# A fused attention and two-layer feed-forward kernel: a second staging buffer for spare weights, and a longer pipeline in the attention's first ten pairs

## The chip, the cores and the metric

The kernel runs on one core of a Trainium2 chip. A core has TensorE (PE: matmuls; PEld are its weight loads), VectorE (DVE), ScalarE (ACT), GpSimd (POOL) and SyncE (SP), which issues all DMAs here. The metric is the device time of one execution in microseconds (us), as the median of some runs.

## What is computed

Windowed attention with bias, then two feed-forward layers, in float32:

```python
scores = q @ k^T / 8 + bias; keep = (8 global keys) | (96 keys before the row)
a = softmax(where(keep, scores, -1e9)); x = a @ v      # 2 x 8 heads, 768 x 64
h = x @ w_in1;  x = (max(h,0) + alpha*min(h,0)) @ w_out1   # 1536 x 512, d_ff 2048
h = x @ w_in2;  out = (P(h) / (Q(h) + 1e-6)) @ w_out2      # P cubic, Q quadratic
```

## The kernel before, in words

**Attention.** A step z (0 to 47) is one block of 128 query rows and two heads, and a pair u (0 to 23) is two steps. A pair goes through these stages: `scores` (TensorE, L423), `biased` (VectorE adds the bias out of PSUM and keeps the row extremes, L440), `exponentials` (ScalarE, with row sums, L450), the reciprocals of the sums (`inverse`, L462: GpSimd adds 1e-9, L464, VectorE inverts, L465), `normalise` (GpSimd scales the probabilities, L470), `transpose_p` (TensorE, L486) and `copy_p` (PSUM to SBUF, L494: VectorE for every fourth step up to step 16, else ScalarE), `values` (TensorE, L505), and `store_x` (ScalarE writes the high part L526, VectorE the low part L527). Probabilities have six buffers (two steps each to three pairs), transposed ones four.

**Order.** All is written out by hand; each engine takes its own instructions in program order. Pairs 0 to 9 run in `alone(u)` (L569): scores u, reciprocals of step 2u-1 (`one_ready`), biased u, loads (`fetches`, SP), values u-2, exponentials of step 2u, store u-2, the transposes and splits of new q and k blocks, reciprocals of step 2u, a tick, exponentials of step 2u+1, transposes and copies of pair u-1, a tick. Pairs 10 to 23 share the engines with the first layer: slot s (0 to 15, `joint_slot`, L848) is pair u = 10 + s. It calls `opening` (L605: scores, reciprocals of pair u-1, biased, loads, values u-2, exponentials, store), then `first(s)` (12 matmuls of 128x512, one PSUM bank), a tick, `turning` (L623: transposes and copies of pair u-1, new inputs), `leaky(s)` (VectorE L744 and L745 read the bank, ScalarE L746, GpSimd L747), `second(s-1)` (12 matmuls) and a tick. Slots from 16 on are feed-forward alone.

**Weights.** Each weight piece (512 KB of 64-bit words) is loaded to a stage, scaled on ScalarE (L324), joined on VectorE (L313 to L315) and split into a high part (L301 on ScalarE in the slots, L303 on GpSimd in `alone`) and a low part (VectorE, L304). `tick` (L284) is one step of that: it issues the DMAs of the piece before (`spill`, L209), casts the high part of the present one and starts the next. A plan fixes at which tick a piece starts. Eight pieces, those of chunks 8 to 11, have no slot in SBUF yet (`slot is None`): they are split into `self.part[1:3]` and sent to DRAM. Their plan numbers are 15 and 17 to 23; one starts in each slot from 5 to 12 and is cast at the end of the slot after, 6 to 13.

```python
self.spill()
x = words(self.dx[n % 3])
if slot is None:
    hi, lo = (t.bitcast(F32R) for t in self.part[1:3])
```

Of the kernel before, what the change touches and what calls it, by code (L numbers as in the profile page):

```python
# [8 lines left out]
F32 = mybir.dt.float32  # L9
F32R = mybir.dt.float32r  # L10
# [3 lines left out]
ALU = mybir.AluOpType  # L14
# [3 lines left out]
P = 128  # L18
# [4 lines left out]
DM = 512  # L23
# [14 lines left out]
JOIN = 20  # L38
# [22 lines left out]
class Kernel:  # L61
# [222 lines left out]
    def tick(self, on_act, start, spread=False):  # L284
        nc = self.nc
        if self.later:
            self.later.popleft()()
        while self.splits:
            self.splits.popleft()()
        self.join_step(5)  # L290
        if self.pipe and self.pipe[0][0] == "joined":
            _, n = self.pipe.popleft()
            m, fc, kind, slot = self.plan[n]
            self.spill()
            x = words(self.dx[n % 3])
            if slot is None:
                hi, lo = (t.bitcast(F32R) for t in self.part[1:3])
            else:
                hi, lo = (flat(self.slots[slot][kind, part]) for part in PARTS)
            if on_act:  # L300
                nc.scalar.copy(hi, x)  # L301
            else:
                nc.gpsimd.tensor_scalar(hi, x, 1.0, 1.0, ALU.mult, ALU.mult)  # L303
            self.splits.append(lambda: nc.vector.tensor_sub(lo, x, hi.bitcast(F32)))  # L304
            if m == 0 and fc < KEPT:
                for part, of in zip(PARTS, (hi, lo)):
                    self.unspilled.append((words(self.spilled[fc][kind, part]), of.bitcast(F32)))
        if self.pipe:
            _, n = self.pipe[0]
            self.pipe[0] = "joined", n  # L310
            low, e, y = self.staged(n)[:, :, :, 0], self.de[n % 2].bitcast(I32), self.dx[n % 3]
            self.join += [
                lambda: nc.vector.tensor_scalar(y, e, 3, None, ALU.logical_shift_left),  # L313
                lambda: nc.vector.scalar_tensor_tensor(y, e, -(2**31), y, ALU.bitwise_and, ALU.bitwise_or),  # L314
                lambda: nc.vector.scalar_tensor_tensor(y, low, 29, y, ALU.logical_shift_right, ALU.bitwise_or),  # L315
                self.load_more,
            ]
        if not spread:
            self.join_step(5)
        if start:  # L320
            n = self.started
            self.started += 1
            self.pipe.append(("scaled", n))
            nc.scalar.mul(self.de[n % 2], self.staged(n)[:, :, :, 1].bitcast(F32), 2.0**-112)  # L324
# [37 lines left out]
    def attention_window(self, pool, moe):  # L362
# [10 lines left out]
        rec = [pool.tile([P, 4], F32, name=f"rec{i}") for i in range(2)]  # L373
        pt = [pool.tile([P, 2, 2, P], F32, name=f"pt{i}") for i in range(4)]
        self.first_saved = [pool.tile([P, DM], F32, name=f"first{d}") for d in range(NC)]

        def load(nm, i):
            if 2 <= i < NBLK:
# [80 lines left out]
                    accum_out=st[:, 4 + j : 5 + j],  # L459
                )  # L460

        def inverse(u, rows):  # L462
            r = rec[u % 2][:, rows]
            nc.gpsimd.tensor_scalar(r, stat[u % 3][:, 4:8][:, rows], 1e-9, 1.0, ALU.add, ALU.mult)  # L464
            nc.vector.reciprocal(r, r)  # L465

        def normalise(z):
            w, p, r, e = width(z), prob[z % 6], rec[z // 2 % 2], 2 * (z % 2)
            for j in range(2):
                nc.gpsimd.tensor_scalar(p[:, j, :w], p[:, j, :w], r[:, e + j : e + j + 1], 1.0, ALU.mult, ALU.mult)  # L470

        def one_ready(z):
            if z >= 0:
                inverse(z // 2, slice(2 * (z % 2), 2 * (z % 2) + 2))
                normalise(z)

        def both_ready(u):
            if steps_of(u):
                inverse(u, slice(0, 4))
                for z in steps_of(u):  # L480
                    normalise(z)

# [3 lines left out]
        def transpose_p(u, first_bank):  # L486
            for z in steps_of(u):
                w, p, t = width(z), prob[z % 6], transposed(z, first_bank + z % 2)
                for j in range(2):
                    nc.tensor.transpose(t[:, j, 0], p[:, j, w - P : w], ident)  # L490
                    if w == WIN:
                        nc.tensor.transpose(t[:, j, 1], p[:, j, 0:P], ident)
# [12 lines left out]
        def values(u):  # L505
            for z in steps_of(u):
                i, c = divmod(z, 4)
                w, p = width(z), pt[z % 4]
                o = vbank[:, c]
                for ch in range(1 if w == P else 2):  # L510
                    for j in range(2):
                        h = 2 * c + j
                        if ch == 0:
                            nc.tensor.matmul(o[HALF[j]], va[i % 4][:, h], p[:, j, 0], start=True, stop=w == P)
                        else:
                            nc.tensor.matmul(
                                o[HALF[j]], vb[i % 3][:, h], p[: NPREV + NG, j, 1], start=False, stop=True
                            )


        def store_x(u):
            if steps_of(u):
                g, off = divmod(u // 2 * P, GT)
                cs = (near, far)[u % 2]
                hi, lo = (x[g][:, cs, off : off + P] for x in (self.xhi, self.xlo))
                nc.scalar.copy(hi, vbank[:, cs])  # L526
                return lambda: nc.vector.tensor_sub(lo, vbank[:, cs], hi.bitcast(F32))  # L527
            return lambda: None
# [13 lines left out]
        def fetches(u):  # L542
            for z in (2 * u, 2 * u + 1):
                for lead, fetch in (
                    (KL, lambda i: load("k", i)),
                    (QL, lambda i: load("q", i)),
                    (VL, load_va),
                    (BL, load_vb),
                ):
                    if (z + lead) % 4 == 0:  # L550
                        fetch((z + lead) // 4)
# [17 lines left out]
        def alone(u):  # L569
            t = 2 * u - JOIN  # L570
            scores(u)
            one_ready(2 * u - 1)
            biased(u)
            if u < 2:
                later_masks(range(4 * u, 4 * u + 4))
                for _ in range(2 * KEEP):
                    nc.tensor.matmul(banks[2][:, 0:P], ident, ident, start=True, stop=True)
            fetches(u)
            values(u - 2)
            exponentials(2 * u)  # L580
            lows = [store_x(u - 2)]
            for n, (nm, i, cs) in enumerate(inputs(u)):
                bank = (3, 2)[n % 2]
                transpose_in(nm, i, bank, cs)
                lows.append(split_in(nm, i, bank, cs))
                if u < 2:
                    lows.pop()()
            keys_of_all(u)
            one_ready(2 * u)
            self.tick(False, t in self.starts, spread=True)  # L590
            exponentials(2 * u + 1)
            transpose_p(u - 1, 6)
            for low in lows:
                low()
            self.join_step(3)
            copy_p(u - 1, 6)
            self.tick(False, t + 1 in self.starts, spread=u < JOIN // 2 - 1)
            if u == 1:
                self.moe_constants()
            if u == 6:  # L600
                self.moe_constants_ready()
            if 2 * u in WL:
                self.load_next()

        def opening(u):  # L605
            scores(u)
            keys_of_all(u)
            if u == JOIN // 2:
                one_ready(2 * u - 1)
            else:  # L610
                both_ready(u - 1)
            biased(u)
            fetches(u)
            values(u - 2)
            some = steps_of(u)
            for z in some[:1]:
                exponentials(z)
            low = store_x(u - 2)
            for z in some[1:]:
                exponentials(z)  # L620
            low()

        def turning(u):  # L623
            transpose_p(u - 1, 0)
            lows = []
            for nm, i, cs in inputs(u):
                transpose_in(nm, i, 2, cs)
            copy_p(u - 1, 0)
            for nm, i, cs in inputs(u):
                lows.append(split_in(nm, i, 2, cs))  # L630
            return lows
# [6 lines left out]
    def attention_any(self, pool, moe):  # L638
# [16 lines left out]
        pt = pool.tile([P, NB, P], F32, name="a_pt")  # L655
        st = pool.tile([P, 4], F32, name="a_st")
        self.first_saved = [pool.tile([P, DM], F32, name=f"a_first{d}") for d in range(NC)]

        def transposed(dst, scale, nm, i):
            self.load_tokens(nm, i, ra)  # L660
# [317 lines left out]
```

## Time and profile before

| | |
|---|---|
| three runs | 677.8 us median (676.52 to 678.18) |
| the profiled execution | 678.08 us, its span 676.2 us |
| busy in the span | PE 631.6 us (93%), DVE 541.6 (80%), ACT 374.7 (55%), POOL 195.2 (29%) |
[...]
| pairs 0 to 9 | first scores at 8.49 us; first scores of slot 0 at 60.47 us |
| slots 9 to 15 | 150.78 to 219.60 us |

The span runs from the first to the last instruction; the execution has 1.88 us around it. Busy time says how full an engine is, not what the others wait for. That is read from the rows in which an instruction names the idle time before it and what ended it, in brackets, and from the chain of work that ended last.

### The profile page before, as it was taken

To read this page: it belongs to the slowest core of one execution; us is meant where nothing else is said; L and a number is where in the kernel's file an instruction comes from. 1 tells how busy PE (TensorE), PEld (TensorE's weight loads), DVE (VectorE), ACT (ScalarE), POOL (GpSimd) and SP (SyncE) were. 2 spreads that over 40 slices of the span, in tenths; PEclk is the share of its full clock that TensorE was granted. 3 is DMA by queue.
4 is the path that set the end of the run, shared out by engine and by line. 5 is a ranking of instruction groups with operands and counts; after the bars stand their busy time and mean duration, and the time that the engine had idled before them with its cause. 6 is when DMAs were issued, how large, how long until landed. Compare 5 with 4: busy or idle time off the path is not lost.

```text
span 676.2 us, 9567 instructions
## 1 busy us (share of the span) xinstructions
PE 631.6 (93%) x3250; PEld 510.2 (75%) x3250; DVE 541.6 (80%) x982; ACT 374.7 (55%) x782; POOL 195.2 (29%) x278
## 2 busy tenths in 40 slices
PE   7767998998988999999999998999999999999994
PEld 6656766776866888888888876888878888888782
DVE  3687789984654998876879999999999877786984
ACT  2775565665552432333324367777777766766662
POOL 4554334333232322222222212222222222222221
PEclk9897999998999999999999999999999999999997
DMA  8969488876667882331342231121110000300302
GB/s 164 198 165 271 136 249 251 258 221 222 186 225 235 291 317 89 99 121 31 126 155 63 70 117 31 32 95 39 55 62 1 1 1 1 124 1 0 126 0 69
DMA packets 84860, 82.83 MB, mean 123 GB/s; under 512 B 45312, under 2 KB 61952, under 8 KB 84800
## 3 DMA queue, kind: packets, MB, share of 16 engines
q1 hardware_dynamic: 84800, 82.11, 40.5%
q8 instruction: 28, 0.46, 0.3%
q14 instruction: 32, 0.26, 0.1%
HBM read 60.21 MB, written 19.92 MB: 119 GB/s over the span
## 4 chain that ended last, share of the span: by engine, by line
PE 59%; DVE 23%; ACT 6%; DMA 4%; issue 3%; POOL 3%; SPq 0%; DVEq 0%; ACTq 0%; POOLq 0%
PE bank L804 29%; PE bank L738 28%; DVE dx L314 3%; DVE dx L315 3%; DVE dx L313 3%; ACT prob L453 2%; DMA dwouthi_f<-part 2%; DVE prob L446 1%; DVE act L745 1%; DVE act L744 1%; DMA dwinhi_f<-part 1%; DVE xlo L527 1%; DVE klo L407 1%; DVE act L782 1%; POOL glo L747 1%
## 5 line engine op out<-in xcount | busy, mean ns | idle before, releaser
L747 POOL TENSOR_TENSOR glo<-act,ghi 128x512 fp32r<-128x512 f32 x48 | 65.6, 1367 | 225.6 <-ACT ghi L746 202.6
L789 POOL TENSOR_TENSOR glo<-act,ghi 128x512 fp32r<-128x512 f32 (+1 forms) x49 | 65.7, 1340 | 202.1 <-ACT ghi L785 187.2
L746 ACT CAST ghi<-act 128x512 fp32r<-128x512 f32 x48 | 29.8, 621 | 107.6 <-DVE act L745 99.7
L738 PE MATMUL bank<-xhi,winhi_f 128*128 128x512 f32 x256 | 68.4, 389 | 0.0
L738 PE MATMUL bank<-xhi,winlo_f 128*128 128x512 f32 x256 | 68.4, 389 | 0.0
L738 PE MATMUL bank<-xlo,winhi_f 128*128 128x512 f32 x256 | 68.4, 389 | 0.0
L453 ACT ACTIVATE prob<-prob,stat 128x232 f32<-128x232 f32 (+1 forms) x96 | 44.6, 466 | 38.8 <-DVE stat L446 38.7
L738 PEld LDWEIGHTS bank<-xhi,winhi_f 128*128 128x128 f32 x256 | 48.0, 188 | 10.0
L738 PEld LDWEIGHTS bank<-xlo,winhi_f 128*128 128x128 f32 x256 | 48.0, 188 | 10.0
L738 PEld LDWEIGHTS bank<-xhi,winlo_f 128*128 128x128 f32 x256 | 48.0, 188 | 10.0
L315 DVE SCALAR_TENSOR_TENSOR dx<-stage,dx 128x512 int32<-128x512 int32 x64 | 53.5, 836 | 2.2
L314 DVE SCALAR_TENSOR_TENSOR dx<-de,dx 128x512 int32<-128x512 int32 x64 | 51.8, 809 | 2.2
L756 ACT ACTIVATE stage<-bank 128x512 f32<-128x512 f32 (+1 forms) x49 | 28.8, 588 | 37.5 <-PE bank L738 37.4
L765 DVE SCALAR_TENSOR_TENSOR stage<-stage,abs_b 128x512 f32<-128x512 f32 (+1 forms) x49 | 36.2, 739 | 16.3 <-ACT stage L757 16.3
L470 POOL TENSOR_SCALAR prob<-prob,rec 128x232 f32<-128x232 f32 (+1 forms) x96 | 43.0, 464 | 21.7 <-DVE rec L465 14.3
L785 ACT CAST ghi<-act 128x512 fp32r<-128x512 f32 (+1 forms) x49 | 30.1, 614 | 26.5 <-DVE act L782 26.4
L324 ACT ACTIVATE de<-stage 128x512 f32<-128x512 f32 x64 | 42.4, 667 | 2.3 <-DMA stage<-in_moe_w_out_dram 2.3
L804 PE MATMUL bank<-wouthi_f,ghi 128*128 128x512 f32 x144 | 41.3, 392 | 0.6 <-ACT ghi L785 0.6
L744 DVE TENSOR_SCALAR act<-bank,al 128x512 f32<-128x512 f32 x48 | 35.8, 745 | 7.4 <-PE bank L738 7.2
L804 PE MATMUL bank<-wouthi_f,glo 128*128 128x512 f32 x144 | 41.2, 391 | 0.1
L804 PE MATMUL bank<-woutlo_f,ghi 128*128 128x512 f32 x144 | 41.0, 389 | 0.0
L313 DVE TENSOR_SCALAR dx<-de 128x512 int32<-128x512 int32 x64 | 38.0, 594 | 3.5 <-ACT de L324 3.5
(206 smaller groups left out, 1483.5 us busy)
## 6 DMA issues: line engine op xcount, KB each, us to landing
stage<-in_moe_w_in_dram SPq DMA_DIRECT2D x32, 512.0 KB, 4.1
stage<-in_moe_w_out_dram SPq DMA_DIRECT2D x32, 512.0 KB, 4.0
part<-saved_f SPq DMA_DIRECT2D x16, 256.0 KB, 4.3
va<-in_v_dram SPq DMA_DIRECT2D x13, 256.0 KB, 5.0
saved_f<-part SPq DMA_DIRECT2D x12, 256.0 KB, 3.7
out_dram<-part SPq DMA_DIRECT2D x11, 256.0 KB, 2.1
rawk<-in_k_dram SPq DMA_DIRECT2D x10, 256.0 KB, 4.7
rawq<-in_q_dram SPq DMA_DIRECT2D x10, 256.0 KB, 4.6
```

Source lines behind the costliest of these rows:

```text
L313: lambda: nc.vector.tensor_scalar(y, e, 3, None, ALU.logical_shift_left),
L314: lambda: nc.vector.scalar_tensor_tensor(y, e, -(2**31), y, ALU.bitwise_and, ALU.bitwise_or),
L315: lambda: nc.vector.scalar_tensor_tensor(y, low, 29, y, ALU.logical_shift_right, ALU.bitwise_or),
L324: nc.scalar.mul(self.de[n % 2], self.staged(n)[:, :, :, 1].bitcast(F32), 2.0**-112)
L453: nc.scalar.activation(p[:, j - e, :w], p[:, j - e, :w], AF.Exp, bias=st[:, j : j + 1], scale=-1.0, accum_out=st[:, 4 + j : 5 + j],)
L470: nc.gpsimd.tensor_scalar(p[:, j, :w], p[:, j, :w], r[:, e + j : e + j + 1], 1.0, ALU.mult, ALU.mult)
L738: nc.tensor.matmul(bk, w["in", a][:, c, :], x[:, c, :], start=e == 0, stop=e == len(seq) - 1)
L744: nc.vector.tensor_scalar(t, h, 0.0, self.al[:, fc : fc + 1], ALU.min, ALU.mult)
L747: nc.gpsimd.tensor_tensor(lo, t, hi.bitcast(F32), ALU.subtract)
L765: nc.vector.scalar_tensor_tensor(w, w, self.ab[:, 0:1], ab, ALU.add, ALU.mult)
L789: nc.gpsimd.tensor_tensor(lo, u, hi.bitcast(F32), ALU.subtract)
L804: nc.tensor.matmul(y[d], lhs, rhs, start=begin and e == 0, stop=last and e == 2)
```

## The change

It gives the spare pieces a second pair of buffers, `self.spare`, chosen by the parity of the plan number n. In `alone(u)` the reciprocals of both steps of pair u-1 are taken together, after scores u; transposes and copies are those of pair u-2, values and stores those of pair u-3, and values stand before the loads. Slot 0 then transposes and copies two pairs (8 and 9; pair 8 through banks 4 and 5), and slot 1 takes the values of two pairs (8 and 9) and stores both.

```diff
             if slot is None:
-                hi, lo = (t.bitcast(F32R) for t in self.part[1:3])
+                hi, lo = (t.bitcast(F32R) for t in (self.part[1:3], self.spare)[n % 2])
...
+        self.spare = [pool.tile([P, DM], F32, name=f"spare{d}") for d in range(2)]
...
-        def inverse(u, rows):
-            r = rec[u % 2][:, rows]
-            nc.gpsimd.tensor_scalar(r, stat[u % 3][:, 4:8][:, rows], 1e-9, 1.0, ALU.add, ALU.mult)
-            nc.vector.reciprocal(r, r)
...
-        def one_ready(z):
-            if z >= 0:
-                inverse(z // 2, slice(2 * (z % 2), 2 * (z % 2) + 2))
-                normalise(z)
...
         def both_ready(u):
             if steps_of(u):
-                inverse(u, slice(0, 4))
+                r = rec[u % 2]
+                nc.gpsimd.tensor_scalar(r, stat[u % 3][:, 4:8], 1e-9, 1.0, ALU.add, ALU.mult)
+                nc.vector.reciprocal(r, r)
...
         def alone(u):
             t = 2 * u - JOIN
             scores(u)
-            one_ready(2 * u - 1)
+            both_ready(u - 1)
             biased(u)
...
+            values(u - 3)
             fetches(u)
-            values(u - 2)
             exponentials(2 * u)
-            lows = [store_x(u - 2)]
+            lows = [store_x(u - 3)]
...
             keys_of_all(u)
-            one_ready(2 * u)
             self.tick(False, t in self.starts, spread=True)
             exponentials(2 * u + 1)
-            transpose_p(u - 1, 6)
+            transpose_p(u - 2, 6)
...
-            copy_p(u - 1, 6)
+            copy_p(u - 2, 6)
...
         def opening(u):
             scores(u)
             keys_of_all(u)
-            if u == JOIN // 2:
-                one_ready(2 * u - 1)
-            else:
-                both_ready(u - 1)
+            both_ready(u - 1)
             biased(u)
+            due = {JOIN // 2: (u - 3,), JOIN // 2 + 1: (u - 3, u - 2)}.get(u, (u - 2,))
+            for v in due:
+                values(v)
             fetches(u)
-            values(u - 2)
...
-            low = store_x(u - 2)
+            lows = [store_x(v) for v in due]
...
         def turning(u):
+            if u == JOIN // 2:
+                transpose_p(u - 2, 4)
             transpose_p(u - 1, 0)
...
+            if u == JOIN // 2:
+                copy_p(u - 2, 4)
             copy_p(u - 1, 0)
```

## Rows read from the trace of the kernel before

**Rows 1.** Chain that ended last, by line, whole span: share of the span.

```profile
PE bank L804 29%; PE bank L738 28%; DVE dx L314 3%; DVE dx L315 3%; DVE dx L313 3%; ACT prob L453 2%; DMA dwouthi_f<-part 2%; DVE prob L446 1%; DVE act L745 1%; DVE act L744 1%; DMA dwinhi_f<-part 1%; DVE xlo L527 1%; DVE klo L407 1%; DVE act L782 1%; POOL glo L747 1%
```

**Rows 2.** ScalarE's waits, 130 to 212 us: total us, times, longest us.

```profile
ACT part L301 <- DMA dwouthi_f<-part: 10.0, 3, 3.5
ACT part L301 <- DMA dwinhi_f<-part: 8.9, 3, 3.0
```

**Rows 3.** Busy us by stretch, slots 9 to 15; last columns TensorE clock, DMA share, GB/s.

```profile
150.78:164.75 13.97, 10.71 (x66) 8.43 (x66) 6.81 (x19) 7.96 (x20) 3.66 (x7) 0.88 0.52 173
164.75:173.65 8.90, 8.90 (x66) 7.30 (x65) 5.33 (x16) 4.79 (x14) 2.83 (x6) 1.00 0.77 253
173.65:182.11 8.46, 8.46 (x62) 6.86 (x61) 4.24 (x15) 4.92 (x14) 3.24 (x6) 1.00 0.73 249
...
213.00:219.60 6.60, 6.60 (x41) 5.47 (x41) 1.87 (x3) 1.38 (x4) 1.52 (x2) 1.00 1.01 337
sum 68.82, PE 61.53 PEld 47.71 DVE 34.05 ACT 32.00 POOL 21.02; mean PE 8.79 PEld 6.82 DVE 4.86 ACT 4.57 POOL 3.00
```

**Rows 4.** ScalarE in order of time, slots 8 to 10: start, us, instruction, [idle before <-releaser].

```profile
156.94 0.62 ACT L301 CAST part<-dx 128x512 fp32r<-128x512 f32 x1 [3.41 <-DMA dwouthi_f<-part]
167.23 0.62 ACT L301 CAST part<-dx 128x512 fp32r<-128x512 f32 x1 [2.98 <-DMA dwinhi_f<-part]
168.31 0.48 ACT L453 ACTIVATE prob<-prob,stat 128x232 f32<-128x232 f32 x1
```

**Rows 5.** VectorE in order of time, slots 10 and 11.

```profile
165.94 0.18 DVE L465 RECIPROCAL rec<-rec 128x4 f32<-128x4 f32 x1 [1.79 <-POOL rec L464]
166.32 0.08 DVE L446 DVE_READ_ACCUMULATOR2_ANT stat<- 128x1 f32 x1
...
176.23 0.18 DVE L465 RECIPROCAL rec<-rec 128x4 f32<-128x4 f32 x1 [1.79 <-POOL rec L464]
```

**Rows 6.** TensorE in order of time, pair 1 and slot 9.

```profile
20.23 0.60 PE L490 MATMUL bank<-part,prob 128*128 128x128 f32 x4
...
159.82 0.66 PE L399 MATMUL bank<-part,rawk 128*128 128x128 f32 x4 [3.26 <-DVE xlo L527]
```

**Rows 7.** GpSimd in order of time, pairs 0 and 1, and slot 0.

```profile
15.69 0.19 POOL L464 TENSOR_SCALAR rec<-stat 128x2 f32<-128x2 f32 x1
16.99 0.19 POOL L464 TENSOR_SCALAR rec<-stat 128x2 f32<-128x2 f32 x1
...
72.36 1.28 POOL L747 TENSOR_TENSOR glo<-act,ghi 128x512 fp32r<-128x512 f32 x1 [8.13 <-ACT ghi L746]
```

**Rows 8.** VectorE in order of time, pairs 1, 2 and 7, and slot 0.

```profile
17.22 0.17 DVE L465 RECIPROCAL rec<-rec 128x2 f32<-128x2 f32 x1 [1.14 <-POOL rec L464]
...
22.95 0.17 DVE L465 RECIPROCAL rec<-rec 128x2 f32<-128x2 f32 x1 [0.82 <-POOL rec L464]
...
46.22 0.17 DVE L465 RECIPROCAL rec<-rec 128x2 f32<-128x2 f32 x1 [0.57 <-POOL rec L464]
...
69.70 0.75 DVE L744 TENSOR_SCALAR act<-bank,al 128x512 f32<-128x512 f32 x1 [3.70 <-PE bank L738]
...
72.41 1.51 DVE L313 TENSOR_SCALAR dx<-de 128x512 int32<-128x512 int32 x1
```

**Rows 9.** ScalarE in order of time, pair 4 and slot 0.

```profile
30.85 0.49 ACT L453 ACTIVATE prob<-prob,stat 128x232 f32<-128x232 f32 x1 [0.48 <-DVE stat L446]
...
70.19 1.07 ACT L501 COPY pt<-bank 128x512 f32<-128x512 f32 x2 [3.14 <-PE bank L492]
```

**Rows 10.** VectorE groups by shape, 20 to 61 us: busy us, mean ns, idle before.

```profile
L501 DVE COPY pt<-bank 128x512 f32<-128x512 f32 x3 | 2.0, 679 | 0.0
L313 DVE TENSOR_SCALAR dx<-de 128x512 int32<-128x512 int32 x4 | 1.6, 408 | 0.0
```

**Rows 11.** Busy us by stretch, 40 us after the attention, columns as in Rows 3.

```profile
216.00:256.00 40.00, 40.00 (x178) 33.14 (x177) 35.57 (x47) 16.00 (x27) 10.49 (x8) 1.00 0.86 302
```

More of the change, by code (lines that the diff above doesn't have):

```diff
@@ L617, in opening @@
                 exponentials(z)
-            low = store_x(u - 2)
+            lows = [store_x(v) for v in due]
             for z in some[1:]:
                 exponentials(z)
-            low()
+            for low in lows:
+                low()
         def turning(u):
+            if u == JOIN // 2:
+                transpose_p(u - 2, 4)
             transpose_p(u - 1, 0)
@@ L657, in attention_any @@
         self.first_saved = [pool.tile([P, DM], F32, name=f"a_first{d}") for d in range(NC)]
+        self.spare = [pool.tile([P, DM], F32, name=f"a_spare{d}") for d in range(2)]
         def transposed(dst, scale, nm, i):
```

## The prediction

> **What bounds it now.** I read the chain of waits first. It is mostly TensorE's two feed-forward lines, but two DMAs stand in it, both out of `part` [rows 1]: the spare pieces on their way to DRAM. The next view, ScalarE's waits, says who feels them. Six casts (L301) stood 18.9 us in all for such a DMA, about 3.1 us each [rows 2]. Eight pieces are cast into the one pair of buffers; the first two find it free, the other six wait.
>
> The third view asks what that costs, slot by slot. Slots 9 to 15 take 68.82 us. In slots 10 and 11 TensorE is busy throughout, 8.90 us with a new input block to transpose and 8.46 without; slot 9 takes 13.97 at a mean granted clock of 0.88 [rows 3]. In slot 9 the cast waits 3.41 us [rows 4], the exponentials and the store queue behind it on ScalarE, and TensorE stands 3.26 us until the store's low part has left the bank [rows 6]. Later the wait sits in a ring: reciprocal, biased, exponentials, store, split, join, `leaky`, L746, L747, GpSimd's sums, next reciprocal. From 165.94 to 176.23 that is 10.29 us [rows 5]. The first row extremes are there at 166.40 [rows 5], the first exponential starts at 168.31, behind the cast that waited 2.98 us [rows 4]: 1.91 us of the ring are the wait, 8.38 are work.
>
> In pairs 0 to 9 VectorE waits for GpSimd's sums ahead of its reciprocals [rows 8]. After slot 15 TensorE is busy 40.00 us of 40 [rows 11], so what the attention saves reaches the end.
>
> **Part 1, the second buffers.** Removed: the wait of casts three to eight. Plan numbers 18 to 23 alternate, so a buffer is used again two slots later. Today's casts wait some 3 us after one slot; one slot more, at least 8.46 us [rows 3], leaves over 5 us. Numbers 15 and 17 share a buffer, as they do now, with another piece between them. Instructions and DMAs stay the same in number. What is late next is TensorE: with the ring at 8.38 us and TensorE at 8.46 or more, I sum TensorE's work. Slots 9 and 10: 8.90 each. Slots 11, 12, 13: 8.46 each. Slot 15: 6.60 [rows 3]. Slot 14 is slot 15 and eight transposes; four early ones took 0.60 [rows 6], so 7.7 at most. Sum 57.4, which is 11.4 less than 68.82. Ring and TensorE are within 0.1 us of each other and hand over to each other, so I give back 0.6: **-10.8**. Ends: if TensorE never stalls, -11.8; if only slot 9 is cured (13.97 against 8.90) and the ring finds another wait as long, -5.1.
>
> **Part 2, the first pairs.** GpSimd sums step 0's columns at 15.69, must scale step 0 and only then sums step 1's, at 16.99 [rows 7]; VectorE's reciprocal follows at 17.22 and pair 1's biased behind it [rows 8]. Both exponentials of pair 0 are done by then, so one sum over four columns can stand at 15.69: -1.3. The same holds for pair 2, whose reciprocal waited 0.82 [rows 8]: -0.8. Together **-2.1**, ends 0 (another wait takes over) and -2.5.
>
> **Part 3, the middle reciprocals.** In each pair VectorE stops once before the join for a reciprocal that follows the exponentials just made: 0.57 us at pair 7 [rows 8], and the instruction itself 0.08 until the next. Both go. In pairs 2 to 5 ScalarE is the bound and its own wait, 0.48 at pair 4 [rows 9], stays, since a reciprocal still stands ahead of biased: worth nothing there. In pairs 6 to 8 weight joins fill VectorE and it pays: 3 x 0.65 = **-1.95**. In pair 9 ScalarE's exponentials and two copies lead to the first values of slot 0 either way: nothing. Ends 0 and -2.6.
>
> **Part 4, what moves into slots 0 and 1.** Slot 0 gets eight more transposes (up to 1.2), a copy on ScalarE (half of 1.07) [rows 9] and one on VectorE (0.68) [rows 10]; slot 1 eight value matmuls, a store and its low part, about 0.4 as half the columns of that copy. VectorE waits 3.70 us for `first(0)` [rows 8], but pair 8's transposes stand behind `first(0)`, so the copy falls into the way of `leaky(0)`. From there to slot 7 VectorE sets the pace, and TensorE's extra work hides in its waits: 0.68 + 0.4, **+1.0**. Ends: 0, and +2.7 with all of it on the path.
>
> **Part 5, queues and ports.** In pairs 6 and 8 the load of an earlier-value tile on SP now waits for values of pair u-3; behind it stand only loads that follow a VectorE join. The copies those values need are a pair old; I cost it at 0, at most 2. GpSimd's four scalings of a pair now lie in one run, beginning beside biased and ending beside the join's first instruction, L313, where before two lay beside the second and third. L313 takes 0.41 us on average in pairs 6 to 9 [rows 10] and took 1.51 in slot 0 [rows 8], where GpSimd's L747 ran beside it for 1.28 [rows 7]. I take 0, because a scaling is a third of L747 and the joins behind are freed; the upper end is three pairs of 1.1, +3.3.
>
> [...]
>
> **The sum.** -10.8 - 2.1 - 1.95 + 1.0 = -13.85. The profiled execution took 678.08 us, so **664.2**; it lies 0.3 above the median of the three runs, inside their spread of 1.7.
>
> **Rivals.**
> 1. *The ring finds another wait.* With ScalarE free, biased waits for GpSimd or `first` for the bank that `leaky` reads, and slots stay near 10.3. For it: 8.38 against 8.46 leaves no room. Against it: nothing in the ring grows. Part 1 falls to -5.1: 669.9.
> 2. *The opening returns its gain.* GpSimd's run of four blocks L313 in pairs 6 to 8, +3.3 as in part 5, so parts 2 to 5 come to nothing: 667.3. For it: the 1.51. Against it: a scaling is far shorter.
> 3. *The buffers do not do it.* The cast would still be late because of the DMAs themselves, or parity would put neighbours together. Only the opening remains: 675.0. Against it: the numbers 18 to 23, and DMA shares of 0.52 to 0.77 in slots 9 to 11, against 1.01 in slot 15 [rows 3].
> [...]
>
> **Chances.** Forecast 0.61, rivals 0.15, 0.14, 0.06, 0.04 in that order. The lower end takes the good ends of all parts, -11.8 - 2.5 - 2.6 - 0 = -16.9, and some more for a copy that hides: 660. The upper end takes in rivals 1 and 2 and their unknown tails: 671.5. Left out are rivals 3 and 4 and the tails, under 0.2. A measurement of this kernel can tell about 0.3%, 2 us, from no change. Slower by more is rival 4 and a remainder, 0.05; within it is a part of rival 3, 0.04; faster 0.91.
>
> **What would show it.** Casts into `part` and `spare` with no DMA named before them; slots 9 to 15 in 57 to 59 us with TensorE busy throughout and reciprocals some 8.5 apart; pair 1's biased before 16.2; one reciprocal a pair, and first scores of slot 0 near 56.5; slot 0 about 1 us longer. Wrong if casts still wait, if reciprocals stay 10 us apart, or if L313 in pairs 6 to 8 takes over 1 us.

## The result, and the profile after

The changed kernel takes **661.82 us** (median of four runs, 661.18 to 663.47) against 677.75 for the kernel before in the same session: a ratio of 0.9772, interval 0.9748 to 0.9795. That is 2.4 us below the forecast and inside its range. The profiled execution took 662.42 us, its span is 660.6: 15.6 us less than before's.

Where the 15.6 went, from the start of the first scores (or values) of each slot in the two traces: 3.37 us are won by the start of slot 9 (150.78 before, 147.41 after), 10.86 us in slots 9 to 15 (68.82 and 57.96), and 1.37 in what follows, where both kernels do the same work. I take that last piece as scatter: it lasted 456.6 us before and 455.2 after, and it lasts 455.4 to 456.6 in the profiles of the twelve experiments below, all with the same work there.

ScalarE's waits from 121 to 206 us (slots 6 to 15, without the first 3 us of slot 6), to be held against [rows 2] (columns: total us, times, longest us):

```profile
ACT ghi L743 <- DVE act L742: 17.8, 9, 4.1
ACT prob L454 <- DVE stat L447: 11.5, 7, 2.7
ACT pt L494 <- PE bank L485: 4.3, 5, 3.1
ACT xhi L519 <- PE bank L509: 2.6, 1, 2.6
```

The two lines with a DMA are gone. The casts alone, in slots 9 to 13:

```profile
L301 ACT CAST part<-dx x3: 613/614/649, 150.0 to 182.8; 128x512 fp32r<-128x512 f32 x3
L301 ACT CAST spare<-dx x3: 612/613/613, 157.3 to 191.4; 128x512 fp32r<-128x512 f32 x3
its engine sat idle before it (us, times) until:
```

They alternate between the two pairs of buffers, and under the line on idle time stands nothing: not one cast waited. What that gives, slot by slot, to be held against [rows 3] (columns: stretch, its length, busy us of PE, PEld, DVE, ACT and POOL, granted TensorE clock with 1.00 for full speed, DMA share, GB/s):

```profile
147.41:156.31 8.90, 8.90 (x65) 7.30 (x64) 5.85 (x18) 7.25 (x19) 3.23 (x6) 1.00 0.67 235
156.31:165.36 9.05, 8.98 (x65) 7.30 (x65) 6.68 (x19) 5.68 (x16) 3.23 (x6) 1.00 0.98 290
165.36:173.83 8.47, 8.47 (x62) 6.86 (x62) 5.93 (x17) 5.05 (x15) 3.23 (x6) 1.00 0.80 257
173.83:182.31 8.48, 8.48 (x62) 6.86 (x62) 5.59 (x16) 5.02 (x15) 3.23 (x6) 1.00 0.72 242
182.31:190.77 8.46, 8.46 (x62) 6.86 (x61) 5.58 (x16) 5.08 (x14) 3.23 (x6) 1.00 0.74 254
190.77:198.77 8.00, 8.00 (x50) 6.08 (x49) 2.71 (x5) 3.13 (x6) 4.95 (x7) 1.00 0.86 292
198.77:205.37 6.60, 6.60 (x42) 5.47 (x41) 1.87 (x3) 1.33 (x3) 0.26 (x1) 1.00 1.00 343
sum 57.96, PE 57.89 PEld 46.72 DVE 34.20 ACT 32.52 POOL 21.37; mean PE 8.27 PEld 6.67 DVE 4.89 ACT 4.65 POOL 3.05
```

In each row the second number equals the first, or nearly: TensorE is busy 57.89 us of 57.96, at full clock. Slot 9 fell from 13.97 us to the 8.90 of a slot with an input block. That is the prediction's picture of part 1. A row that reads as full can still hide a little waiting: experiment 6 does slot 14's work in 7.60 us, not 8.00.

The first pairs on VectorE (start us, us; idle before and its releaser in brackets), to be held against [rows 8]:

```profile
16.00 0.18 DVE L472 RECIPROCAL rec<-rec 128x4 f32<-128x4 f32 x1 [1.36 <-POOL rec L471]
16.10 0.26 DVE L447 CUSTOM_DVE_ANT_0 prob<-bank,bm 128x128 f32<-128x128 f32 x1
...
19.20 0.69 DVE L408 TENSOR_TENSOR klo<-bank,khi 128x512 fp32r<-128x512 f32 x1 [2.20 <-ACT khi L407]
19.81 0.68 DVE L411 SCALAR_TENSOR_TENSOR qlo<-bank,qhi 128x512 fp32r<-128x512 f32 x1
21.26 0.69 DVE L408 TENSOR_TENSOR klo<-bank,khi 128x512 fp32r<-128x512 f32 x1 [0.77 <-ACT khi L407]
22.31 0.18 DVE L472 RECIPROCAL rec<-rec 128x4 f32<-128x4 f32 x1 [0.36 <-POOL rec L471]
```

Pair 1's biased stands at 16.10, 1.2 us earlier than before, as said. But then VectorE waits 2.20 us for the split of new keys, and pair 2's biased comes at 22.41, only 0.63 earlier than before's 23.04. ScalarE in turn waits for TensorE's transposes:

```profile
18.59 0.58 ACT L407 CAST khi<-bank 128x512 fp32r<-128x512 f32 x1 [1.30 <-PE bank L400]
```

What makes those late is TensorE's clock, which the windows of 2 us show (columns as above):

```profile
12.00:14.00 2.00, 1.77 (x9) 1.36 (x7) 0.22 (x1) 0.57 (x2) 0.93 (x4) 0.50 1.35 221
14.00:16.00 2.00, 1.76 (x13) 1.65 (x14) 0.63 (x2) 0.95 (x5) 1.64 (x11) 0.50 0.51 105
16.00:18.00 2.00, 2.00 (x10) 2.00 (x11) 1.00 (x9) 0.88 (x4) 1.64 (x5) 0.50 1.00 242
```

At 0.50 eight idle matmuls that both kernels have there (L570) take 2.07 us and the eight input transposes behind them 1.37, where before's took 1.16 and 1.04 at 1.00. So they run into 19 us, and ScalarE has nothing to split. The profiled execution of the kernel before had 1.00 in the same stretch, and so had some of the profiles below: this term differs from execution to execution.

Slot 0 was to become 1 us longer and became 2.95 us shorter (10.44 before, 7.49 after). That is counted from scores to scores; 1.6 of it lie in where the slot is taken to begin, since its scores ran 2.61 us ahead of its biased before and run 0.97 ahead after. Counted on VectorE, from biased to biased, slot 0 went from 12.30 to 11.05 us. The rows of slot 0's biased and `leaky(0)` on VectorE, and of its first values and `first(0)` on TensorE:

```profile
60.31 0.40 DVE L447 CUSTOM_DVE_ANT_0 prob<-bank,bm 128x232 f32<-128x232 f32 x1 [0.44 <-PE bank L432]
...
65.20 0.69 DVE L494 COPY pt<-bank 128x512 f32<-128x512 f32 x1 [2.62 <-PE bank L485]
65.80 0.74 DVE L741 TENSOR_SCALAR act<-bank,al 128x512 f32<-128x512 f32 x1
...
68.39 1.51 DVE L313 TENSOR_SCALAR dx<-de 128x512 int32<-128x512 int32 x1
```

```profile
60.20 0.44 PE L507 MATMUL bank<-pt,va 128*64 128x128 f32 x4
...
62.74 1.07 PE L735 MATMUL bank<-xhi,winlo__112 128*128 128x512 f32 x4
63.65 1.07 PE L735 MATMUL bank<-xlo,winhi__111 128*128 128x512 f32 x4
```

Before, biased, the first values and the same matmuls of `first(0)`:

```profile
63.08 0.38 DVE L446 CUSTOM_DVE_ANT_0 prob<-bank,bm 128x232 f32<-128x232 f32 x1
```

```profile
63.15 0.69 PE L514 MATMUL bank<-pt,va 128*64 128x128 f32 x4 [1.75 <-DVE pt L501]
...
66.93 1.81 PE L738 MATMUL bank<-xhi,winlo__112 128*128 128x512 f32 x4
68.58 1.08 PE L738 MATMUL bank<-xlo,winhi__111 128*128 128x512 f32 x4
```

The copy of pair 8 does stand ahead of `leaky(0)`, as part 4 said, and costs it 1.04 us: 0.60 for itself and 0.44 because it waits for its transposes. `leaky(0)` starts 1.24 us after the last matmul of `first(0)` has given way to transposes (at 64.56); before it started 0.20 us after (at 69.50), and so it does in experiment 4, which moves the copy. But four matmuls that took 1.81 us take 1.07: the values and `first(0)` together fell from 6.35 us to 4.36, and the clock over them is 1.00 where it was 0.58. The windows give the clock in steps of 5 us, the kernel before first:

```profile
60.00:65.00 5.00, 3.25 (x31) 2.52 (x30) 3.85 (x16) 3.64 (x13) 2.51 (x7) 0.67 1.02 299
65.00:70.00 5.00, 5.00 (x19) 4.01 (x18) 0.72 (x2) 1.88 (x6) 0.00 (x0) 0.65 0.25 58
```

```profile
55.00:60.00 5.00, 4.76 (x39) 4.13 (x40) 4.17 (x15) 3.52 (x12) 3.18 (x7) 0.66 0.99 337
60.00:65.00 5.00, 4.79 (x39) 3.61 (x36) 1.79 (x9) 3.08 (x11) 1.76 (x4) 1.00 0.94 233
65.00:70.00 5.00, 4.60 (x56) 4.06 (x56) 4.22 (x6) 3.13 (x6) 1.53 (x2) 1.00 0.00 0
```

The stretch at some 0.66 has moved from slot 0, where TensorE sets the end, into pair 9, where (experiment 11) VectorE does.

### The profile page after: what moved, and what is told of

Read it like the earlier page. It is cut to its first block, busy times and chain, and to the rows that moved or that the text cites. A ratio compares the mean times of both kernels' runs of the same rounds, so it can differ in the third digit from the quotient of the medians.

```text
span 660.6 us, 9551 instructions
## 1 busy us (share of the span) xinstructions
PE 622.9 (94%) x3250; PEld 506.3 (77%) x3250; DVE 541.1 (82%) x972; ACT 374.8 (57%) x782; POOL 191.6 (29%) x268
## 5 line engine op out<-in xcount | busy, mean ns | idle before, releaser
L744 POOL TENSOR_TENSOR glo<-act,ghi 128x512 fp32r<-128x512 f32 x48 | 65.6, 1366 | 213.5 <-ACT ghi L743 193.8
L315 DVE SCALAR_TENSOR_TENSOR dx<-stage,dx 128x512 int32<-128x512 int32 x64 | 52.1, 815 | 2.2
L313 DVE TENSOR_SCALAR dx<-de 128x512 int32<-128x512 int32 x64 | 38.6, 603 | 3.5 <-ACT de L324 3.5
L777 DVE SCALAR_TENSOR_TENSOR stage<-stage,cq,bank 128x512 f32<-128x512 f32 (+1 forms) x49 | 36.0, 734 | 4.1 <-ACT bank L767 4.1
```

What stands on the lines that cost most here:

```text
L744: nc.gpsimd.tensor_tensor(lo, t, hi.bitcast(F32), ALU.subtract)
L777: nc.vector.scalar_tensor_tensor(w, w, self.cq[:, 0:1], r, ALU.add, ALU.mult)
```

## The experiments

The theory: part 1 is worth 10.8 us because slots 9 to 15 leave the DMA's waits and become bound by TensorE; the opening is worth some 3 us, and its odd terms are TensorE's clock. Runs of one group share a chip and the runs of the kernel before: 677.09 us for experiments 1 to 4, 678.65 for 5 to 8, 677.50 for 9 to 12.

**1 and 2. Each half alone.** Kernel 1 is the kernel before with the spare buffers; kernel 2 is the changed kernel, which has the spare buffers but doesn't use them:

```diff
-                hi, lo = (t.bitcast(F32R) for t in (self.part[1:3], self.spare)[n % 2])
+                hi, lo = (t.bitcast(F32R) for t in self.part[1:3])
```

> The kernel before with the second pair of buffers alone. Theory (parts add up): the casts wait for no DMA, slot 9 still starts at 150.8 us, slots 9 to 15 take 58 us in place of 68.8, the time is about 666.9 us (10.9 less). Rival (the buffers pay only beside the new opening, because the ring of slots 9 to 15 finds another wait): slots 9 to 15 at 63 us or more, 672 us.

> The changed kernel with the one old pair of buffers. Theory: slot 9 starts 3.4 us earlier than before, six casts wait 3 us each again, slots 9 to 15 take 68.8 us, the time is about 674.3 us. Rival (the order of the opening also shortens slots 9 to 15): below 672 us. Rival (the opening is worth nothing by itself): 677 us or more.

Kernel 1: 667.50 us, 0.9858 (0.9842 to 0.9873); slots 9 to 15 take 58.25 us at clock 1.00 and start at 150.80, where they did before. Kernel 2: 673.62 us, 0.9951 (0.9936 to 0.9966); slot 9 starts at 145.99, and ScalarE waits as before:

```profile
ACT part L301 <- DMA dwouthi_f<-part: 9.6, 3, 3.4
ACT part L301 <- DMA dwinhi_f<-part: 8.9, 3, 3.1
```

Each half does its own part. The product of the ratios is 0.9810, beside 0.9772 for both: some 2.6 us more together, by medians. By stages the halves add up: slots 9 to 15 take 58.25 us in kernel 1 and 57.96 in the changed kernel, and slot 9 starts at 145.99 in kernel 2 and, in a profile of the changed kernel with pair 1 at the same clock (experiment 9), at 146.31. So the profiles show no gain that needs both; what the medians differ by stays open.

**3. The reciprocals alone.** Kernel 1 and the joint reciprocals, with the old lag of transposes and values:

```diff
-            one_ready(2 * u - 1)
+            both_ready(u - 1)
             biased(u)
...
-            one_ready(2 * u)
...
-            if u == JOIN // 2:
-                one_ready(2 * u - 1)
-            else:
-                both_ready(u - 1)
+            both_ready(u - 1)
```

> The second buffers, and the reciprocals of a pair taken together after the next pair's scores; transposes, copies, values and stores at their old lag, so nothing moves into slots 0 and 1. Theory (the lag of the transposes is there to keep TensorE fed and its clock up): pair 9's transposes wait some 2 us for GpSimd, first(0) runs at the lower level in about 4.5 us against 3.3, and this eats the 1.2 us of VectorE work that slots 0 and 1 are spared: 661.5 to 663.5 us. Rival (the moved work is a cost and buys nothing): about 660.6 us.

663.60 us, 0.9791 (0.9777 to 0.9804): 3.9 us of the opening's gain come with the reciprocals. TensorE does wait now, in pair 9, for the pair's scaled probabilities:

```profile
PE bank L491 <- POOL prob L471: 3.1, 3, 2.8
```

A lower clock is still there when slot 0 begins, at a mean of 0.78 in the slot:

```profile
60.08:67.75 7.67, 7.67 (x53) 6.46 (x52) 3.61 (x13) 4.31 (x14) 1.97 (x5) 0.78 0.69 177
```

Its values take 0.60 to 0.69 us for four matmuls, as in the kernel before, but `first(0)` behind them takes 1.07 for four, as it does at 1.00 in the changed kernel. So the expectation that `first(0)` would take some 4.5 us failed, it took 2.85: the joint reciprocals alone move the slow stretch out of `first(0)`. In the changed kernel, with the longer lag, the values are fast too (0.39 to 0.44 for four). Slot 1 takes 10.11 us, 0.65 less than in the changed kernel, which is the price of the second store moved there. Slot 9 starts at 147.63, beside 147.41 in the changed kernel; pair 1's eight idle matmuls took 2.07 us in both profiles, 1.16 before. What the longer lag of transposes and values brings is within 2 us and not settled.

**4. Pair 8's copy on ScalarE**, so that it no longer stands ahead of `leaky(0)`:

```diff
-                copy = nc.vector.tensor_copy if z < JOIN - 3 and z % 4 == 0 else nc.scalar.copy
+                copy = nc.vector.tensor_copy if z < JOIN - 4 and z % 4 == 0 else nc.scalar.copy
```

> The changed kernel with the copy of step 16 in slot 0 on ScalarE in place of VectorE. Theory (VectorE sets the pace from slot 0 to slot 7): leaky(0) starts 0.6 us earlier after first(0) and slot 9 about 0.5 us earlier, 661.3 us. Rival (ScalarE's four copies in a row then delay the new queries, the scores of slot 1 and VectorE with them): 661.8 us or a little more.

662.11 us, 0.9783 (0.9769 to 0.9797): no gain. `leaky(0)` starts as soon as `first(0)` is done, 1.04 us sooner behind it than in the changed kernel, and VectorE then waits for ScalarE, which has four copies instead of three ahead of the new queries:

```profile
64.23 0.69 DVE L742 SCALAR_TENSOR_TENSOR act<-bank,act 128x512 f32<-128x512 f32 x1
66.47 0.69 DVE L411 SCALAR_TENSOR_TENSOR qlo<-bank,qhi 128x512 fp32r<-128x512 f32 x1 [1.54 <-ACT qhi L410]
```

**5. The clock of slot 0, in the kernel before.** Twenty idle matmuls in pair 9, between the transposes of its two transposed steps, and nothing else:

```diff
+                if z == JOIN - 4:
+                    for _ in range(20):
+                        nc.tensor.matmul(banks[7][:, 0:P], ident, ident, start=True, stop=True)
```

> The kernel before with 20 idle matmuls of 128x128 on TensorE in pair 9, between the transposes of steps 16 and 17, where it waits 2.35 us for GpSimd. Theory (the shorter slot 0 of the changed kernel comes from TensorE's clock): first(0) runs in 3.0 to 3.4 us in place of 4.5, slot 0 is 1.3 to 1.7 us shorter, 676.3 us. Rival (the clock has nothing to do with it, or falls again before first(0)): slot 0 as before, 677.8 us.

675.13 us, 0.9953 (0.9940 to 0.9967), some 3 us, more than expected. Slot 0 falls from 10.44 to 6.28 us:

```profile
60.00:65.00 5.00, 4.94 (x53) 4.35 (x52) 4.20 (x18) 4.08 (x16) 2.77 (x7) 1.00 1.05 313
65.00:70.00 5.00, 4.95 (x35) 3.98 (x33) 2.26 (x4) 3.72 (x11) 0.00 (x0) 1.00 0.29 64
```

Pairs 8 and 9 grow by 1.67 us (the idle matmuls themselves take some 4.6), and 2.2 are left at slot 2. Slot 9 stalled at clock 1.00 here and took 12.38 us instead of 13.97, but slot 10 gave 1.44 of that back (10.34 and 8.90), as in kernel 2. So work that does nothing shortens the kernel before: the clock of slot 0 was worth as much there as part 2 was to bring.

**6, 7 and 8. What bounds slots 9 to 15.** The changed kernel with two more matmuls in each of slots 9 to 13 (6), with `leaky`'s first operation done twice there (7), and with neighbours sharing a buffer, three waits instead of none (8). Kernels 6 and 7 only add work.

```diff
+            for c in range(2) if CH < n < CH + 6 else ():
+                nc.tensor.matmul(bk, w["in", "hi"][:, c, :], self.xhi[g][:, c, :], start=True, stop=True)
```

```diff
             nc.vector.tensor_scalar(t, h, 0.0, self.al[:, fc : fc + 1], ALU.min, ALU.mult)
+            if CH < n < CH + 6:
+                nc.vector.tensor_scalar(t, h, 0.0, self.al[:, fc : fc + 1], ALU.min, ALU.mult)
```

```diff
-                hi, lo = (t.bitcast(F32R) for t in (self.part[1:3], self.spare)[n % 2])
+                hi, lo = (t.bitcast(F32R) for t in (self.part[1:3], self.spare)[n // 2 % 2])
```

> The changed kernel with two more 128x512 matmuls (0.45 us) ahead of first(s) in slots 9 to 13. Theory (TensorE is the bound of these slots): each is 0.45 us longer, 2.3 us in all, 664.1 us. Rival (VectorE's ring or the DMAs set 8.47 us and TensorE only follows): at most 0.5 us more, 662.3 us or less.

> The changed kernel with the first instruction of leaky done twice in slots 9 to 13 (0.7 us more on VectorE in the ring). Theory (the ring is within 0.1 us of TensorE, 8.4 against 8.47): it becomes 9.1 us, slots 11 to 13 grow by 0.6 each and 9 and 10 by 0.2, some 2.2 us in all, 664.0 us. Rival (TensorE alone is the bound, the ring has 0.7 us to spare): no change, 661.8 us.

> The changed kernel with the buffer chosen by n // 2 % 2, so that plan numbers 19, 21 and 23 share a buffer with the number before them. Theory (each wait lengthens the ring by 1.9 us, of which a slot without one wins back 0.1): three casts wait 3 us, two ring turns of about 10.3 us and a last one half as dear, 4 to 5 us more, 666.2 us. Rival (a slot without a wait absorbs it): at most 1 us more, 662.8 us.

Kernel 6: 665.29 us, 0.9811 (0.9795 to 0.9827). Slots 9 to 13 grow by 0.32 to 0.46 us each, about what two matmuls take (four in 1.07 or less), and TensorE stays full, as in slot 9:

```profile
146.66:156.02 9.36, 9.36 (x68) 7.68 (x68) 6.30 (x19) 7.30 (x20) 3.23 (x6) 1.00 0.69 234
```

Slot 14 gives 0.40 back (7.60 us), so slots 9 to 15 take 59.70 us, 1.74 more, where 2.3 were expected.

Kernel 7: 666.78 us, 0.9826 (0.9811 to 0.9841). Slots 9 to 15 take 61.93 us, 3.97 more, for five operations of some 0.75: the whole of it, where 2.2 were expected. On TensorE it comes late, two thirds of it in slots 13 and 14 and none in slot 9, which was not expected. In the ring it comes evenly, as the distances of the six reciprocals show (us):

| kernel | 9 to 10 | 10 to 11 | 11 to 12 | 12 to 13 | 13 to 14 |
|---|---|---|---|---|---|
| changed | 9.18 | 8.50 | 8.49 | 8.55 | 8.55 |
| 6, more on TensorE | 9.18 | 8.50 | 8.52 | 8.58 | 8.85 |
| 7, more on VectorE | 9.97 | 9.28 | 9.29 | 9.36 | 9.35 |

Kernel 6 hardly stretches the ring, though TensorE's slots 11 to 13 take 8.92 or 8.93 us there. So a ring turn is some 8.5 us by itself, just above TensorE's 8.46, and work added to either comes out at the end: 1.74 of some 2.1 us in kernel 6, all of it in kernel 7. The prediction had 8.38 and 8.46.

Kernel 8: 665.90 us, 0.9812 (0.9797 to 0.9827), slots 9 to 15 in 60.84 us, 2.88 more:

```profile
ACT spare L301 <- DMA dwinhi_f<-spare: 5.7, 2, 2.9
ACT part L301 <- DMA dwinhi_f<-part: 2.7, 1, 2.7
```

Where a buffer is used again one slot later the wait is back, 2.7 to 2.9 us, and where two slots later it isn't. That is the mechanism of part 1, in the number of waits asked for. The 2.88 us are below the theory's 4 to 5. The wait that stalled slot 9 in the kernel before (13.97 us, 8.90 here) is not among these three, which are those of numbers 19, 21 and 23. The other five waits cost 5.8 us before, in slots 10 to 15; three of them cost half of that here, and a slot without a wait between two that have one makes up part of it (8.63 and 8.48 us in slots 11 and 12, behind 10.26 in slot 10).

**9 to 12. The clock in pairs 1 and 9 of the changed kernel.** Kernel 9 is the changed kernel again; 10 has more idle matmuls at the start, 11 has twenty in pair 9 ahead of its values, 12 has both.

```diff
-WARM, KEEP = 9, 2
+WARM, KEEP = 21, 2
...
+            if u == JOIN // 2 - 1:
+                for _ in range(20):
+                    nc.tensor.matmul(banks[7][:, 0:P], ident, ident, start=True, stop=True)
             values(u - 3)
```

> The changed kernel once more, as the base of the three beside it. Both theories: 661 to 663.5 us, with pair 1 at a granted clock of 0.50 in 10 to 18 us in some executions and at 1.00 in others. It also answers how often: if the profiled execution has first scores of pair 2 near 19.1 it ran warm, near 20.5 cold.

> The changed kernel with 21 idle matmuls instead of 9 ahead of the first transposes, so that TensorE stands less before them (1.85 us in the changed kernel). Theory (part 2 fell short because pair 1 ran at the lower clock level): granted clock 1.00 from 10 to 18 us, first scores of pair 2 near 19.1 instead of 20.54, and a median 0.5 to 1.3 us below the changed kernel's. Rival (the clock at the start is decided elsewhere, or the gain is lost behind ScalarE by pair 5): pair 2 at 20.5, or slot 0 at the same time as before, and the same median within 0.4 us.

> The changed kernel with 20 idle matmuls in pair 9 ahead of the values, where TensorE stands 4.03 us and then does values and transposes at a granted clock of 0.66. Theory (the clock in pair 9 costs): transposes of pair 9 0.27 us each instead of 0.42, first scores of slot 0 1 to 2 us earlier, median 0.5 to 1.5 us below the changed kernel's. Rival (VectorE sets the pace of pairs 8 and 9, it is busy without a gap from 45.3 to 57.3): slot 0's scores earlier, but leaky of slot 0 at the same time, and the same median within 0.4 us; if the idle matmuls themselves run at the lower level they end after 55.2 and cost up to 1.

> Both fillings together. Theory: the gains of the two add, 1 to 2.8 us below the changed kernel, 659 to 661 us. Rival: what pair 1 wins is lost before pair 9, and the time is that of the better of the two alone.

| kernel | median (range), us | ratio to before | pair 2, slot 0, slot 9 start at |
|---|---|---|---|
| 9 changed again | 662.30 (661.68 to 663.51) | 0.9778 (0.9765 to 0.9792) | 19.16, 58.23, 146.31 |
| 10 start filled | 661.07 (660.83 to 661.94) | 0.9756 (0.9743 to 0.9769) | 18.20, 57.61, 145.92 |
| 11 pair 9 filled | 662.74 (661.98 to 663.72) | 0.9785 (0.9771 to 0.9798) | 19.16, 57.94, 146.28 |
| 12 both | 661.14 (660.99 to 661.80) | 0.9757 (0.9744 to 0.9771) | 17.93, 56.76, 145.13 |

The profiled execution of kernel 9 happened to run pair 1 at full clock, and is the changed kernel's other face: pair 2 starts at 19.16 instead of 20.54, slot 9 at 146.31 instead of 147.41. From 10 to 20 us, kernel 9 and then the profile of the changed kernel shown above:

```profile
10.00:20.00 10.00, 8.20 (x64) 7.06 (x64) 4.19 (x22) 4.95 (x18) 7.33 (x27) 1.00 0.97 169
```

```profile
10.00:20.00 10.00, 8.56 (x49) 7.69 (x49) 3.67 (x21) 4.36 (x16) 7.32 (x27) 0.59 1.00 168
```

The ten runs of kernels 10 and 12 lie between 660.83 and 661.94 us, the ten of 9 and 11 between 661.68 and 663.72: filling the start takes 1.2 to 1.6 us off the median, and kernels 10 and 12 are the fastest versions found, ahead of the changed kernel. Kernel 12 is no faster than 10, so the two fillings don't add up. That pair 1's clock goes with the time up to slot 9 is borne out by the other profiles with this opening and the old start: slot 9 begins at 147.4 to 148.2 us in the three that had 0.50 from 12 to 18 us (the changed kernel, 7 and 8), and at 146.0 to 146.7 in the five that had 1.00 (2, 4, 6, 9 and 11). That it is also what kernels 10 and 12 win isn't shown: only one execution of each kernel was profiled, and 9's and 10's were both at full clock there, 0.2 us apart in time.

Filling pair 9 brings nothing. Its clock rises as meant, from 0.72 to 1.00:

```profile
55.00:60.00 5.00, 5.00 (x48) 4.33 (x46) 4.03 (x17) 4.11 (x13) 3.18 (x7) 0.72 1.05 363
```

```profile
55.00:60.00 5.00, 4.64 (x59) 3.92 (x59) 3.78 (x17) 4.25 (x13) 2.84 (x7) 1.00 1.08 370
```

(kernel 9, then kernel 11), and `leaky(0)` is held back by the same copy, at 64.08 us in both. Ahead of slot 0's biased VectorE waits 0.62 us for GpSimd's sums and 0.15 for the scores in kernel 9, 0.61 and nothing in kernel 11, and that biased starts at 59.20 and 59.19. The 0.72 of TensorE in pair 9 lies beside VectorE's work and cost nothing here (medians of 662.30 us for kernel 9 and 662.74 for 11).

## Why the prediction held, point by point

**Part 1 (-10.8): right, in size and in reason.** 10.86 us measured, slot for slot as summed: 8.90, 9.05, 8.47, 8.48, 8.46, 8.00, 6.60 against 8.90, 8.90, 8.46 three times, 7.7 and 6.60. The 0.6 given back for the tie of ring and TensorE was spent mostly in slots 10 and 14; 0.1 of it is a slip, since slot 14 from its own terms (6.60 and twice 0.60) is 7.8, not 7.7. Reciprocals stand 8.5 us apart and wait for GpSimd's sums, 12.5 us over six, with little effect on TensorE (0.4 us in slot 14). Experiment 8 shows the wait and the distance that removes it, 6 and 7 the tie, with the ring, and not TensorE, the longer by a hair. Rivals 1 and 3 fall with it, and the kernel isn't slower, for which rival 4 had a chance of 0.04: clock 1.00 in all seven slots.

**Part 2 (-2.1): mis-sized in the profiled run.** The wait for the second sum went, but the next one, for the split of new keys, took over: -0.57 at pair 6. That was near the lower end, 0, "another wait takes over". The step that failed took TensorE's clock in pair 1 as in the one profile seen. In kernel 9, the changed kernel with pair 1 at full clock as in the profile before, biased of pair 6 starts at 36.77 us, against 38.46 before: -1.69, near the forecast. Slot 9 then lies 4.47 us earlier than before, 1.1 more than in the profile shown.

**Part 3 (-1.95): right.** Biased was 0.57 us earlier than before at pair 6 and 2.88 at pair 9: -2.31. VectorE's waits for sums between 24 and 60 us fall from 6.5 us, eleven times, to 3.0, five times:

```profile
  POOL rec L464: 6.5, 11
```

```profile
  POOL rec L471: 3.0, 5
```

(under the reciprocals' line, before and after).

**Part 4 (+1.0): its terms too small, its stage wrong.** The copy costs 1.04 ahead of `leaky(0)`, where 0.68 was its own time and its wait for the transposes was left out; the moved store costs 0.66 in slot 1 (10.10 before, 10.76 after), against 0.4: +1.70. What failed besides is the sentence "slot 0 about 1 us longer": the slot was priced at before's clock, 0.67. `leaky(0)` gained 1.13 us on the biased of slot 0 in spite of the copy, and 1.99 us came from the values and `first(0)` at full clock. All the profiles with joint reciprocals have slot 0 at 7.5 to 7.8 us, and the two with the old ones and no filling at 10.44. First scores of slot 0, forecast near 56.5, stood at 59.34: its biased came 2.77 us earlier than before, but its scores, which no longer run so far ahead of it, only 1.13.

So the opening's sum (-3.05 predicted, -3.37 measured) is right partly by accident: part 2 gave 1.5 less in this profile, the moved work cost 0.7 more, and the clock of the values and `first(0)` gave 2.0 that no part had. Of the 2.4 us between forecast and median, 1.4 is the scatter from slot 16 on, 0.4 parts 1 to 5, and 0.6 the distance of the profiled execution from the median.

**Part 5 (0): nearly.** In pairs 6 to 9 L313 rose from 0.41 us to a median of 0.58:

```profile
L313 DVE TENSOR_SCALAR dx<-de x4: 417/578/615, 39.2 to 52.7; 128x512 int32<-128x512 int32 x4
```

Three instructions beside GpSimd's four scalings cost 0.14 to 0.20 us more each, not the 1.1 that rival 2 needed; slot 0's 1.51 beside GpSimd's L744 (the L747 of before) is unchanged. So L313 took up to 0.2 us more beside operations of 0.46, and 1.1 more beside one of 1.28. SP's wait for values ahead of the earlier-value loads is there (2.8 us, once, L389), and no wait for those loads followed on TensorE.

## What to carry to other kernels

Where a cast or copy waits for a DMA that reads its output buffer, look at how many stages later the buffer is used again and how long the DMA is late: one more buffer in turn removed the whole wait here (18.9 us of six casts), and the gain ended where the next limits stood, so add up the next engine's work in a slot and the ring of hand-overs before the change. Price a stage that follows a stall of TensorE at both clocks that the traces show (the same four matmuls of `first(0)` took 1.81 us at 0.52 and 1.07 at 1.00 here), since the new order ahead of slot 0 moved the slow stretch out of it. Idle matmuls paid where TensorE set the pace right behind them (some 3 us in the kernel before) and brought nothing where another engine did (pair 9 of the changed kernel).

## What was not expected of the hardware

One and the same program gets different clocks in different executions: pair 1 ran from 10 to 20 us at a granted 0.59 in one profile of the changed kernel and at 1.00 in another, and slot 9 started 1.1 us later in the first. Nor did the lower clock stay with a stage: the new order of the opening moved a stretch at some 0.66 out of slot 0 into pair 9 and took 2.0 us off slot 0's values and `first(0)`, without one instruction of `first(0)` being touched. Where the casts wait, slot 9's clock matters less than it seems: at 1.00 (kernels 2 and 5) instead of 0.88 the slot is 1.6 us shorter, and the next one 1.3 to 1.4 longer.
